# Turning the exponentials of a top-k attention with a transposing DMA in place of TensorE

## The chip, the cores and the metric

The kernel runs on one core of one Trainium2 chip. A core has five engines, each with its own queue of instructions that it works off in order: PE (TensorE, matrix products into PSUM), DVE (VectorE), ACT (ScalarE), POOL (GpSimd) and SP (SyncE, which here only issues transfers). Engines wait for each other through semaphores; sixteen DMA engines move data between the device's memory and the on-chip SBUF. The metric is device time in microseconds (us) of the core, as the median of several runs.

## The reference: what is computed

Two blocks follow each other. The first is attention with 8 batches, 8 heads, 576 rows and a head size of 64, in which each row keeps only its 32 largest scores. The second is a feed-forward block on the 4608 rows of 512 that the first one leaves.

```python
scores = (q @ k.T) / 8                         # per batch and head, 576 x 576
kth    = the 32nd largest score of each row
scores = where(scores >= kth, scores, -1e9)
attn   = exp(scores - max of the row)
attn   = attn / (sum of the row + 1e-9)
x      = attn @ v                              # heads side by side: 4608 x 512
h      = x @ w_in                              # 4608 x 2048
g      = h * sigmoid(1.702 * h)
out    = g @ w_out                             # 4608 x 512
```

All of it is float32.

## The kernel before

The work of the attention is cut into 144 *slots*. A slot is 128 rows of one pair of heads (two tiles of 128 x 576 scores), or, twice per batch, the last 64 rows of two pairs of heads. Each slot goes through these steps: scores on PE; copy to SBUF on ACT; the 32 largest of each row on DVE, in four rounds of eight (8 MAX8 and 6 MATCH_REPLACE8 instructions, 14 in all, over 576 elements each); two small operations for the thresholds on POOL; a Prelu that removes what lies below the threshold, and an Exp that also sums the row, on ACT; the reciprocal on DVE and the division on ACT and POOL; the turning of the 128 x 1152 exponentials on PE, because the product with v needs the keys on the partitions; the product with v on PE. The result, brought from PSUM to SBUF by ACT, is a piece of `xT`. When `xT` has its four pieces (four slots), it goes through the feed-forward block in four groups: `hidden` on PE, `tanh` on ACT, `gate` on POOL, `project` on PE. After the fourth group ACT writes the output tile `ob`, which a DMA stores.

```python
def topk(n):                # returns 14 DVE operations: MAX8 x2, (MATCH_REPLACE8 x2, MAX8 x2) x3
    ...
def bounds(n):              # two small POOL operations: cut, low
    ...
def exponentials(n, between=lambda: None):
    for i in range(2):
        nc.scalar.activation(sc[:, i, :], sc[:, i, :], AF.Prelu, bias=cut[:, i : i + 1], alpha=HUGE)
    between()
    for i in range(2):
        nc.scalar.activation(pr[:, i * S : (i + 1) * S], sc[:, i, :], AF.Exp, bias=low[:, i : i + 1],
                             accum_out=den[:, i : i + 1])

def divide(n):
    nc.vector.tensor_scalar_add(some[:], den[:], 1e-9)
    nc.vector.reciprocal(rden[:], some[:])
    if n < SETTLED:         # SETTLED = 11: the first slots divide while turning
        ...
    else:
        nc.scalar.activation(pr[:, 0:S], pr[:, 0:S], AF.Copy, scale=rden[:, 0:1])
        nc.gpsimd.tensor_scalar(pr[:, S : 2 * S], pr[:, S : 2 * S], rden[:, 1:2], None, op0=ALU.mult)

def turn(n, first, cols, blocks):      # 4 + 4 + 1 blocks per slot
    tp = ps_t.tile([P, 512], F32, name="tp")
    for c in range(blocks):
        nc.tensor.transpose(tp[:, c * P : (c + 1) * P], pr[:, at], ident[:])      # n >= SETTLED
    nc.scalar.copy(out=to, in_=tp[:, 0 : blocks * P])

def hidden():               # PE, 16 products of 128x128 (two passes each): ph <- win, xT
    ...
def tanh(aside):            # ACT: th <- tanh(ph); aside: h <- ph as well, which frees ph
    ...
def gate(aside):            # POOL, two operations (DVE, one, if not aside); takes the newest: gated.pop()
    ...
def project(blocks):        # PE, up to 4 products of 128x512 (two passes each): po += wout, gT
    ...
    if blocks[-1] == G - 1 and g == NG - 1:
        ob = osp.tile([P, C], F32, name="ob")
        nc.scalar.mul(out=ob[:], in_=po[:], mul=0.5 / RAISE**2)
        for on, to in rows:
            nc.sync.dma_start(to, ob[on, :])

# [...]
def two_slots(n):           # from slot 12 on; program order is the order in each engine's queue
    def find(m):
        for i, op in enumerate(topk(m) if live(m) else [lambda: None] * 14):
            op()
            if i == 5 and live(m - 1):
                divide(m - 1)
    def middle(m):
        if len(to_project) > 3:
            project(range(G))
        go = may_project(2 if n < N else 0)
        if go:
            project(range(G - 1))
        turn_main(m)                      # two groups of four blocks
        if go:
            project(range(G - 1, G))
        turn_ends(m)                      # the ninth block

    begin(first)                          # loads
    soften(n - 1)                         # bounds + exponentials
    bring_all()
    tanh(aside)
    find(n)
    gate(aside)
    prepare_some()                        # turns freshly loaded q or k: PE, then ACT
    middle(n - 2)
    hidden()
    begin(second)
    soften(n)
    tanh(aside)
    gate(aside)
    prepare_some()
    middle(n - 1)
    find(n + 1)
    prepare_some()
    for m in (n + 2, n - 2, n - 1, n + 3):
        if m > n: scores(m); copy_scores(m)
        else:     values(m)               # product with v on PE, then ACT brings it to xT
    prepare_some()
    hidden()
```

Buffers that matter: `ph` (the PSUM of `hidden`) has one, the score PSUM holds one slot, the `tp` PSUM (also used by `values` and `prepare`) has two, `pt` (the turned exponentials) two, `sc` (scores in SBUF) three, `pr` two.

Of the kernel before, what the change touches and what calls it, by code (L numbers as in the profile page):

```python
# [11 lines left out]
F32 = mybir.dt.float32  # L12
U32 = mybir.dt.uint32
I32 = mybir.dt.int32
PSUM = bass.MemoryType.PSUM

P = 128
TOPK = 32
# [10 lines left out]
def kernel(  # L29
# [42 lines left out]
    NPIECE = CC * DFF // PIECE + FC  # L72

    FIRST = (TAIL, 0)
    MAIN = (0, FULL + 2 * TAIL)
    SCALE = 1.0 / float(D) ** 0.5


# [11 lines left out]
    loads = pool("loads", 2)  # L90
    vals = pool("vals", 6)
    qkt = pool("qkt", 6)
    scp = pool("scp", 3)
    prp = pool("prp", 2)
    lefts = pool("lefts", 1)
    small = pool("small", 4)
    ptp = pool("ptp", 2)
    dgp = pool("dgp", 1)
    xtp = pool("xtp", 2)
    xtt = pool("xtt", 1)  # L100
    gtp = pool("gtp", 4)
    thp = pool("thp", 2)
    osp = pool("osp", 1)
    ps_s = pool("ps_s", 2, space=PSUM)
    ps_t = pool("ps_t", 2, space=PSUM)
    ps_h = pool("ps_h", 1, space=PSUM)
# [189 lines left out]
    def divide(n):  # L296

        den, pr = st[n]["den"], st[n]["pr"]
        some = small.tile([P, 2], F32, name="some")
        nc.vector.tensor_scalar_add(some[:], den[:], 1e-9)  # L300
        rden = small.tile([P, 2], F32, name="rden")
        nc.vector.reciprocal(rden[:], some[:])
        if n < SETTLED:
            by = st[n]["by"] = dgp.tile([P, 2, P], F32, name="by")
            for i in range(2):
                nc.gpsimd.tensor_scalar(by[:, i, :], ident[:], rden[:, i : i + 1], None, op0=ALU.mult)
        else:
            nc.scalar.activation(pr[:, 0:S], pr[:, 0:S], AF.Copy, scale=rden[:, 0:1])
            nc.gpsimd.tensor_scalar(pr[:, S : 2 * S], pr[:, S : 2 * S], rden[:, 1:2], None, op0=ALU.mult)  # L309

    def turn(n, first, cols, blocks):
        pr = st[n]["pr"]
        if first == 0:
            st[n]["pt"] = ptp.tile([P, 2 * NF + 1, P], F32, name="pt")
        to = st[n]["pt"][:, first : first + blocks, :].rearrange("p c r -> p (c r)")
        tp = ps_t.tile([P, 512], F32, name="tp")
        for c in range(blocks):
            at = slice(cols + c * P, cols + (c + 1) * P)
            if n >= SETTLED:
                nc.tensor.transpose(tp[:, c * P : (c + 1) * P], pr[:, at], ident[:])  # L320
            elif first < 2 * NF:
                nc.tensor.matmul(tp[:, c * P : (c + 1) * P], lhsT=pr[:, at], rhs=st[n]["by"][:, first // NF, :])  # L322
            else:
                for i in range(2):
                    nc.tensor.matmul(
                        tp[i * TAIL : (i + 1) * TAIL, 0:P],
                        lhsT=pr[:, cols + i * TAIL : cols + (i + 1) * TAIL],
                        rhs=st[n]["by"][:, i, :],
                    )
        nc.scalar.copy(out=to, in_=tp[:, 0 : blocks * P])  # L330

    def turn_main(n):
        for i in range(2):
            turn(n, i * NF, MAIN[i], NF)

    def turn_ends(n):

        turn(n, 2 * NF, FULL, 1)

    xts = {}  # L340

    def values(n, put_off=None):

        b, t, hps = slots[n]
        pt = st[n]["pt"]
        outs = []
        for p in range(2 if t == NF else 1):
            cols = slice(p * TAIL, (p + 1) * TAIL) if t == NF else slice(0, P)
            main, tail = vv[b, hps[p]]
            o = ps_t.tile([P, 512], F32, name="o", tag="tp")  # L350
            for c in range(NF + 1):
                for j in range(2):
                    nc.tensor.matmul(  # L353
                        o[j * D : (j + 1) * D, 0 : cols.stop - cols.start],
                        lhsT=main[:, j, c, :] if c < NF else tail[:, j, :],
                        rhs=pt[:, j * NF + c if c < NF else 2 * NF, cols],
                        start=(c == 0),
                        stop=(c == NF),
                    )
            outs.append((o, hps[p]))  # L360
        st[n].clear()

        def bring():
            for o, hp in outs:
                if t < NF:
                    if (b, t) not in xts:
                        xts[b, t] = xtp.tile([P, CC, P], F32, name="xT")
                    nc.scalar.copy(out=xts[b, t][:, hp, :], in_=o[:, 0:P])
                else:
                    if (b // 2, t) not in xts:  # L370
                        xts[b // 2, t] = xtt.tile([P, CC, P], F32, name="xT_t")
                    at = b % 2 * TAIL
                    nc.scalar.copy(out=xts[b // 2, t][:, hp, at : at + TAIL], in_=o[:, 0:TAIL])
            if hps[-1] == NP - 1:
                if t < NF:
                    to = out[b * S : b * S + FULL, :].rearrange("(p t) c -> p t c", t=NF)[:, t, :]
                    ready.append((xts.pop((b, t)), [(slice(0, P), to)]))
                elif b % 2:
                    first = [(b - 1 + i) * S + FULL for i in range(2)]
                    rows = [(slice(i * TAIL, (i + 1) * TAIL), out[x : x + TAIL, :]) for i, x in enumerate(first)]  # L380
                    ready.append((xts.pop((b // 2, t)), rows))

        if put_off is None:
            bring()
        else:
            put_off.append(bring)
# [40 lines left out]
    def gate(aside):  # L427
        if not gated:
            return
        th, h, g, rows = gated.pop()  # L430
        gT = gtp.tile([P, G, P], F32, name="gT")
        if aside:
            nc.gpsimd.tensor_scalar(th[:], th[:], 1.0, None, op0=ALU.add)  # L433
            nc.gpsimd.tensor_tensor(out=gT[:], in0=th[:], in1=h[:], op=ALU.mult)  # L434
        else:
            nc.vector.scalar_tensor_tensor(
                out=gT[:], in0=th[:], scalar=1.0, in1=h[:], op0=ALU.add, op1=ALU.mult
            )
        to_project.append((gT, g, rows))

    def project(blocks):

# [9 lines left out]
                po[:], lhsT=gT[:, i, :], rhs=wout[:, f, :], start=(f == 0), stop=(f == FC - 1)  # L452
            )
        if blocks[-1] == G - 1 and g == NG - 1:
            ob = osp.tile([P, C], F32, name="ob")
            nc.scalar.mul(out=ob[:], in_=po[:], mul=0.5 / RAISE**2)  # L456
            for on, to in rows:
                nc.sync.dma_start(to, ob[on, :])
# [7 lines left out]

    READY = (((-9, -8), (-7, -6), (-4, -3), (-2, -1)), ((-7, -6), (-4, -3), (-3, -2), (-1, -2)))
    FETCH = (((-13, -12), (-11, -10), (-7, -7), (-5, -4)), ((-11, -10), (-9, -8), (-5, -5), (-2, -2)))  # L470
    VALUES = ((-8, -7, 0, 0), (-8, -7, 2, 2))
    by_slot = dict(enumerate([2, 2, 3, 3, 3, 3, 3, 3, 3, 3, 2, 2]))
    for n in by_slot:
        first = sum(map(len, list(by_slot.values())[:n]))
# [179 lines left out]
    def two_slots(n):  # L654
# [11 lines left out]
        def prepare_some():  # L666
            for args in preparing.pop(0):
                prepare(*args)
# [3 lines left out]

        def soften(m):
            if live(m):
                bounds(m)
                exponentials(m)

        def find(m):
            for i, op in enumerate(topk(m) if live(m) else [lambda: None] * 14):
                op()  # L680
                if i == 5 and live(m - 1):
                    divide(m - 1)
                if i > 1 and unfinished:
                    finish_one()

        def middle(m):
            if len(to_project) > 3:
                project(range(G))
            go = may_project(2 if n < N else 0)
            if go:  # L690
                project(range(G - 1))
            if live(m) and "pr" in st[m]:
                turn_main(m)
            if go:
                project(range(G - 1, G))
            if live(m) and "pr" in st[m]:
                turn_ends(m)

        begin(first)
        soften(n - 1)  # L700
        bring_all()
        tanh(aside)
        find(n)
        gate(aside)
        prepare_some()
        middle(n - 2)
        hidden()
        begin(second)
        soften(n)
        tanh(aside)  # L710
        gate(aside)
        prepare_some()
        middle(n - 1)
        find(n + 1)
        prepare_some()
        for m in (n + 2, n - 2, n - 1, n + 3):
            if m > n and live(m):
                scores(m)
                copy_scores(m)
            elif m < n and live(m) and "pt" in st[m]:  # L720
                values(m)
        prepare_some()
        hidden()

    with tc.manual_schedule():
        opening()
        for n in range(SETTLED + 1):
            slot(n)
        for n in range(SETTLED + 1, N + 1, 2):
            two_slots(n)  # L730
        while ready or to_gate or gated or to_project:
            last_slot()
# [30 lines left out]
```

## Time and profile before

The median of three runs is 1610.22 us (1610.13 to 1610.37). The profiled execution spans 1608.6 us at a mean granted TensorE clock of 0.990.

| stretch of the profile | span, us | PE busy | DVE busy | ACT busy | POOL busy |
|---|---|---|---|---|---|
| whole | 1608.6 | 1579.4 | 1471.5 | 1152.5 | 748.0 |
| 400 to 1500 us (steady) | 1100.0 | 1099.5 | 1042.4 | 794.0 | 502.4 |

Busy times overlap, as the engines work beside each other. A matmul is pipelined and its recorded time contains its latency, so a PE that is busy all the time has not necessarily been asked for all it could do; weight loads (PEld) stand for the moment at which PE takes up a matmul. The *releaser* of an idle time is the instruction whose semaphore ended it. Line numbers (L260 and so on) are those of the kernel before.

### The profile page before, as it was taken

The page shows a single profiled execution, that of the slowest core. Times are in us where ns is not written, and L with a number is a line of the kernel's source. Part 1 is how long each engine was busy: PE and PEld are TensorE (multiplying, and loading weights), DVE is VectorE, ACT ScalarE, POOL GpSimd, SP SyncE. Part 2 cuts the span into 40 slices and gives each one's busy share as a digit, 9 for nine tenths or more (in the row PEclk, how much of TensorE's full clock was granted, in tenths as well). Part 3 has the DMA queues.
Part 4 walks back from the last instruction along what each step waited for, and adds up shares of the span by engine and source line. Part 5 has one row for each costly group of instructions (what it writes and reads, how often), then busy time and mean ns, then how long its engine had stood idle before and what let it go on. Part 6 is the DMA issues. An engine that isn't in the chain of part 4 may idle for free.

```text
span 1608.6 us, 32167 instructions
## 1 busy us (share of the span) xinstructions
PE 1579.4 (98%) x12045; PEld 1181.2 (73%) x12045; DVE 1471.5 (91%) x3218; ACT 1152.5 (72%) x2442; POOL 748.0 (46%) x780
## 2 busy tenths in 40 slices
PE   7789999999999999999999999999999999999999
PEld 6666777777777777777777777777777777777776
DVE  7999999999999989999999999999999999999960
ACT  7998777777777777677776777677766777677751
POOL 3887444444444444444344444444444444444430
PEclk7899999999999999999999999999999999999999
DMA  7341111110001001110001000001000100000000
GB/s 238 126 158 50 26 30 30 25 35 3 21 15 45 22 23 30 30 43 17 22 15 45 22 23 29 22 21 34 15 23 15 44 23 23 23 8 8 8 8 14
DMA packets 99100, 56.61 MB, mean 35 GB/s; under 512 B 81536, under 2 KB 90240, under 8 KB 98944
## 3 DMA queue, kind: packets, MB, share of 16 engines
q1 hardware_dynamic: 98512, 54.25, 11.9%
q8 instruction: 95, 1.56, 0.4%
q14 instruction: 61, 0.50, 0.1%
q10 hardware_dynamic: 432, 0.30, 0.1%
HBM read 45.09 MB, written 9.44 MB: 34 GB/s over the span
## 4 chain that ended last, share of the span: by engine, by line
PE 93%; DVE 4%; ACT 3%; POOL 0%; issue 0%; POOLq 0%; ACTq 0%
PE ph L403 32%; PE po L451 31%; PE s_ps L240 10%; PE o L353 10%; PE tp L320 8%; DVE top L260 2%; PE tp L208 2%; DVE left L263 1%; ACT sc L251 1%; PE tp L322 1%; ACT pr L291 0%; PE none L168 0%; ACT raw L152 0%; DVE win L151 0%; ACT pt L330 0%
## 5 line engine op out<-in xcount | busy, mean ns | idle before, releaser
L260 DVE MAX8 top<-left 128x8 f32<-128x576 f32 x864 | 609.4, 747 | 0.0
L451 PE MATMUL po<-wout,gT 128*128 128x512 f32 x1152 | 540.4, 593 | 1.2 <-ACT ob L456 0.7
L403 PEld LDWEIGHTS ph<-xT,win 128*128 128x128 f32 x4096 | 467.7, 192 | 41.2 <-issue 40.5
L403 PE MATMUL ph<-xT,win 128*128 128x128 f32 x4096 | 484.3, 276 | 0.0
L263 DVE MATCH_REPLACE8 left<-top,left 128x576 f32<-128x576 f32 x576 | 423.5, 743 | 0.0
L309 POOL TENSOR_SCALAR pr<-pr,rden 128x576 f32<-128x576 f32 x133 | 230.0, 1729 | 351.4 <-ACT th L420 346.2
L451 PEld LDWEIGHTS po<-wout,gT 128*128 128x128 f32 x1152 | 197.6, 191 | 147.3 <-issue 144.5
L330 ACT COPY pt<-tp 128x512 f32<-128x512 f32 (+1 forms) x432 | 193.1, 481 | 148.6 <-PE tp L320 143.1
L433 POOL TENSOR_SCALAR th<-th 128x512 f32<-128x512 f32 x131 | 196.0, 1496 | 220.8 <-ACT th L420 220.8
L288 ACT ACTIVATE sc<-sc,cut 128x576 f32<-128x576 f32 x288 | 208.1, 773 | 119.5 <-POOL cut L279 119.3
L251 ACT COPY sc<-s_ps 128x576 f32<-128x576 f32 x288 | 169.8, 643 | 70.0 <-PE s_ps L240 69.7
L291 ACT ACTIVATE pr<-sc,low 128x576 f32<-128x576 f32 x288 | 219.1, 764 | 0.0
L320 PEld LDWEIGHTS tp<-ident,pr 128*128 128x128 f32 x1197 | 143.1, 141 | 102.0 <-issue 57.1
L263 DVE MATCH_REPLACE8 left<-top,sc 128x576 f32<-128x576 f32 x288 | 211.6, 742 | 0.0
L260 DVE MAX8 top<-sc 128x8 f32<-128x576 f32 x288 | 202.1, 743 | 2.2 <-ACT sc L251 2.2
L240 PE MATMUL s_ps<-k_t,q_t 64*128 64x288 f32 (+1 forms) x1280 | 183.4, 433 | 0.2 <-ACT k_t L210 0.2
L320 PE MATMUL tp<-ident,pr 128*128 128x128 f32 x1197 | 174.2, 273 | 0.0
L434 POOL TENSOR_TENSOR gT<-th,h 128x512 f32<-128x512 f32 x131 | 167.2, 1276 | 10.9
L353 PE MATMUL o<-pt,v_l 128*64 128x128 f32 (+1 forms) x2560 | 158.3, 267 | 0.7
L353 PEld LDWEIGHTS o<-pt,v_l 128*64 128x64 f32 x2560 | 130.8, 137 | 32.6 <-ACT pt L330 13.5
L240 PEld LDWEIGHTS s_ps<-k_t,q_t 64*128 64x128 f32 (+1 forms) x1280 | 100.0, 179 | 59.4 <-issue 41.5
L279 POOL TENSOR_SCALAR cut<-top 128x2 f32<-128x2 f32 x144 | 39.5, 275 | 219.1 <-DVE top L260 219.1
(66 smaller groups left out, 1166.7 us busy)
## 6 DMA issues: line engine op xcount, KB each, us to landing
q_l<-in_q_dram SPq DMA_DIRECT2D x64, 128.0 KB, 2.9
raw<-in_moe_w_in_dram SPq DMA_DIRECT2D x16, 512.0 KB, 4.7
v_l<-in_v_dram SPq DMA_DIRECT2D x32, 256.0 KB, 3.0
raw<-in_moe_w_out_dram SPq DMA_DIRECT2D x16, 512.0 KB, 3.3
out_dram<-ob SPq DMA_DIRECT2D x32, 256.0 KB, 2.3
k_l<-in_k_dram SPq DMA_DIRECT2D x62, 128.0 KB, 2.9
ends<-in_q_dram SPq DMA_DIRECT2D x32, 32.0 KB, 2.4
v_e<-in_v_dram SPq DMA_DIRECT2D x64, 16.0 KB, 2.5
```

Source lines behind the costliest of these rows:

```text
L240: nc.tensor.matmul(ps[i][rows, c, 0:HALF], lhsT=qT[b, hps[p]][on, cols], rhs=kT[b, hps[p]][on, FIRST[i] + c * HALF : FIRST[i] + (c + 1) * ...
L260: nc.vector.max(top[:, i, 8 * r : 8 * r + 8], (left if r else sc)[:, i, :])
L263: nc.vector.match_replace(left[:, i, :], top[:, i, 8 * r : 8 * r + 8], (left if r else sc)[:, i, :], LOWEST)
L288: nc.scalar.activation(sc[:, i, :], sc[:, i, :], AF.Prelu, bias=cut[:, i : i + 1], alpha=HUGE)
L291: nc.scalar.activation(pr[:, i * S : (i + 1) * S], sc[:, i, :], AF.Exp, bias=low[:, i : i + 1], accum_out=den[:, i : i + 1],)
L309: nc.gpsimd.tensor_scalar(pr[:, S : 2 * S], pr[:, S : 2 * S], rden[:, 1:2], None, op0=ALU.mult)
L320: nc.tensor.transpose(tp[:, c * P : (c + 1) * P], pr[:, at], ident[:])
L330: nc.scalar.copy(out=to, in_=tp[:, 0 : blocks * P])
L353: nc.tensor.matmul(o[j * D : (j + 1) * D, 0 : cols.stop - cols.start], lhsT=main[:, j, c, :] if c < NF else tail[:, j, :], rhs=pt[:, j * N ...
L403: nc.tensor.matmul(ph[:, i, :], lhsT=win[:, c, f * P : (f + 1) * P], rhs=xT[:, c, :], start=(c == 0), stop=(c == CC - 1),)
L433: nc.gpsimd.tensor_scalar(th[:], th[:], 1.0, None, op0=ALU.add)
L451: nc.tensor.matmul(po[:], lhsT=gT[:, i, :], rhs=wout[:, f, :], start=(f == 0), stop=(f == FC - 1))
```

## The change

From slot 11 on PE turns nothing any more. ACT splits each float32 exponential into its two 16-bit halves (the tile of the scores, no longer needed, takes them), a DMA writes the halves to device memory, and a second, transposing DMA, which works on 16-bit elements, reads them back turned: rows alternate between low and high halves, so that the turned pairs stand side by side as float32 again. The purpose is to take the turning off PE and its copies from PSUM off ACT, and to leave the transfers, which are long, two slots of time. Around this the program order of the two-slot loop, the loading times and the buffers were rearranged:

```diff
         else:
-            nc.scalar.activation(pr[:, 0:S], pr[:, 0:S], AF.Copy, scale=rden[:, 0:1])
-            nc.gpsimd.tensor_scalar(pr[:, S : 2 * S], pr[:, S : 2 * S], rden[:, 1:2], None, op0=ALU.mult)
+            for i in range(2):
+                on = slice(i * S, (i + 1) * S)
+                nc.gpsimd.tensor_scalar(pr[:, on], pr[:, on], rden[:, i : i + 1], None, op0=ALU.mult)
 ...
+    def turn_by_dma(n):
+        pr, sc = st[n]["pr"], st[n]["sc"]
+        halves = sc[:].rearrange("p i k -> p (i k)").bitcast(U16).rearrange("p (h k) -> p h k", h=2)
+        nc.scalar.copy(out=halves, in_=pr[:].bitcast(U16).rearrange("p (k h) -> p h k", h=2))
+        rows = apart.tile([P, 2, 2 * S], U16, name="rows")
+        nc.sync.dma_start(rows[:], halves)
+        pt = st[n]["pt"] = ptp.tile([P, 2 * NF + 1, P], F32, name="pt")
+        nc.sync.dma_start_transpose(out=pt[:].bitcast(U16), in_=rows[:].rearrange("q h k -> (q h) k"))
 ...
-        th, h, g, rows = gated.pop()
+        th, h, g, rows = gated.pop(0)
 ...                                        # gate writes into th, no gT; ob shares the buffers of th
         def find(m):
             ...
-                if i == 5 and live(m - 1):
+                if i == 6 and live(m - 1):
                     divide(m - 1)
-        def middle(m): ...
+        def project_one():
+            if may_project(0):
+                project(range(G))
+        def measure(m):
+            if live(m):
+                bounds(m)
+            gate(aside)

         begin(first)
+        project_one()
+        measure(n - 1)
         soften(n - 1)                      # now the exponentials alone
         bring_all()
         tanh(aside)
+        if live(n + 2):
+            scores(n + 2)
+            copy_scores(n + 2)
+        brought = []
+        for m in (n - 4, n - 3):
+            if live(m) and "pt" in st[m]:
+                values(m, brought)
+        if live(n + 3):
+            scores(n + 3)
         find(n)
-        gate(aside)
+        if live(n - 1):
+            turn_by_dma(n - 1)
+        for bring in brought:
+            bring()
+        hidden()
         prepare_some()
-        middle(n - 2)
-        hidden()
+        prepare_some()
         begin(second)
+        project_one()
+        measure(n)
         soften(n)
         tanh(aside)
-        gate(aside)
+        if live(n + 3):
+            copy_scores(n + 3)
         prepare_some()
-        middle(n - 1)
-        find(n + 1)
-        prepare_some()
-        for m in (n + 2, n - 2, n - 1, n + 3): ...
         prepare_some()
         hidden()
+        find(n + 1)
+        if live(n):
+            turn_by_dma(n)
```

`sc` goes from three buffers to four and `th` from two to five; the pools of `gT`, `ob` and the first slots' `by` are given up; `pt` keeps its two buffers, and four tiles of `rows` lie in device memory. READY, FETCH and VALUES, the slots at which q, k and v are loaded and prepared, move by up to three slots, so that nearly all `prepare` calls fall on the two in the middle of a pair of slots. The loop runs two pairs further, to slot 147.

More of the change, by code (lines that the diff above doesn't have):

```diff
@@ L14 @@
 I32 = mybir.dt.int32
+U16 = mybir.dt.uint16
 PSUM = bass.MemoryType.PSUM
+DRAM = bass.MemoryType.DRAM
 P = 128
@@ L74 @@
     FIRST = (TAIL, 0)
-    MAIN = (0, FULL + 2 * TAIL)
+    MAIN = (0, NF + 1)
     SCALE = 1.0 / float(D) ** 0.5
@@ L92 @@
     qkt = pool("qkt", 6)
-    scp = pool("scp", 3)
+    scp = pool("scp", 4)
     prp = pool("prp", 2)
@@ L97 @@
     ptp = pool("ptp", 2)
-    dgp = pool("dgp", 1)
     xtp = pool("xtp", 2)
     xtt = pool("xtt", 1)
-    gtp = pool("gtp", 4)
-    thp = pool("thp", 2)
-    osp = pool("osp", 1)
+    thp = pool("thp", 5)
+    apart = pool("apart", 4, space=DRAM)
     ps_s = pool("ps_s", 2, space=PSUM)
@@ L303, in divide @@
         if n < SETTLED:
-            by = st[n]["by"] = dgp.tile([P, 2, P], F32, name="by")
+            by = st[n]["by"] = xtt.tile([P, 2, P], F32, name="by", tag="xT_t")
             for i in range(2):
@@ L307, in divide, with turn @@
         else:
-            nc.scalar.activation(pr[:, 0:S], pr[:, 0:S], AF.Copy, scale=rden[:, 0:1])
-            nc.gpsimd.tensor_scalar(pr[:, S : 2 * S], pr[:, S : 2 * S], rden[:, 1:2], None, op0=ALU.mult)
-    def turn(n, first, cols, blocks):
+            for i in range(2):
+                on = slice(i * S, (i + 1) * S)
+                nc.gpsimd.tensor_scalar(pr[:, on], pr[:, on], rden[:, i : i + 1], None, op0=ALU.mult)
+    def turn(n, first, blocks):
         pr = st[n]["pr"]
@@ L317, in turn @@
         for c in range(blocks):
[L318 to L322, printed above, removed]
+            at = (first + c) * P
+            if first != NF:
+                by = st[n]["by"][:, first // NF, :]
+                nc.tensor.matmul(tp[:, c * P : (c + 1) * P], lhsT=pr[:, at : at + P], rhs=by)
             else:
@@ L326, in turn @@
                         tp[i * TAIL : (i + 1) * TAIL, 0:P],
-                        lhsT=pr[:, cols + i * TAIL : cols + (i + 1) * TAIL],
+                        lhsT=pr[:, at + i * TAIL : at + (i + 1) * TAIL],
                         rhs=st[n]["by"][:, i, :],
@@ L333, in turn_main @@
         for i in range(2):
-            turn(n, i * NF, MAIN[i], NF)
+            turn(n, MAIN[i], NF)
     def turn_ends(n):
-        turn(n, 2 * NF, FULL, 1)
+        turn(n, NF, 1)
+    def turn_by_dma(n):
[6 more added lines that the diff above has]
+        nc.sync.dma_start_transpose(out=pt[:].bitcast(U16), in_=rows[:].rearrange("q h k -> (q h) k"))
     xts = {}
@@ L355, in values @@
                         lhsT=main[:, j, c, :] if c < NF else tail[:, j, :],
-                        rhs=pt[:, j * NF + c if c < NF else 2 * NF, cols],
+                        rhs=pt[:, MAIN[j] + c if c < NF else NF, cols],
                         start=(c == 0),
@@ L429, in gate @@
             return
-        th, h, g, rows = gated.pop()
-        gT = gtp.tile([P, G, P], F32, name="gT")
+        th, h, g, rows = gated.pop(0)
         if aside:
             nc.gpsimd.tensor_scalar(th[:], th[:], 1.0, None, op0=ALU.add)
-            nc.gpsimd.tensor_tensor(out=gT[:], in0=th[:], in1=h[:], op=ALU.mult)
+            nc.gpsimd.tensor_tensor(out=th[:], in0=th[:], in1=h[:], op=ALU.mult)
         else:
             nc.vector.scalar_tensor_tensor(
-                out=gT[:], in0=th[:], scalar=1.0, in1=h[:], op0=ALU.add, op1=ALU.mult
+                out=th[:], in0=th[:], scalar=1.0, in1=h[:], op0=ALU.add, op1=ALU.mult
             )
-        to_project.append((gT, g, rows))
+        to_project.append((th, g, rows))
     def project(blocks):
@@ L454, in project @@
         if blocks[-1] == G - 1 and g == NG - 1:
-            ob = osp.tile([P, C], F32, name="ob")
+            ob = thp.tile([P, C], F32, name="ob", tag="th")
             nc.scalar.mul(out=ob[:], in_=po[:], mul=0.5 / RAISE**2)
@@ L464, in at @@
         later.setdefault(n, []).append((fn, args))
-    READY = (((-9, -8), (-7, -6), (-4, -3), (-2, -1)), ((-7, -6), (-4, -3), (-3, -2), (-1, -2)))
-    FETCH = (((-13, -12), (-11, -10), (-7, -7), (-5, -4)), ((-11, -10), (-9, -8), (-5, -5), (-2, -2)))
-    VALUES = ((-8, -7, 0, 0), (-8, -7, 2, 2))
+    READY = (((-9, -8), (-7, -6), (-4, -3), (-2, -1)), ((-8, -7), (-6, -5), (-4, -3), (-4, -3)))
+    FETCH = (((-13, -12), (-11, -10), (-7, -7), (-5, -4)), ((-12, -11), (-10, -9), (-6, -6), (-5, -5)))
+    VALUES = ((-8, -7, 2, 2), (-8, -7, 3, 3))
     by_slot = dict(enumerate([2, 2, 3, 3, 3, 3, 3, 3, 3, 3, 2, 2]))
@@ L674, in soften @@
             if live(m):
-                bounds(m)
                 exponentials(m)
@@ L684, in find @@
                     finish_one()
-        def middle(m):
-            if len(to_project) > 3:
+        def project_one():
+            if may_project(0):
                 project(range(G))
[L689 to L697, printed above, removed]
+        def measure(m):
+            if live(m):
+                bounds(m)
+            gate(aside)
         begin(first)
+        project_one()
+        measure(n - 1)
         soften(n - 1)
@@ L702, in two_slots @@
         tanh(aside)
-        find(n)
-        gate(aside)
+        if live(n + 2):
[7 more added lines that the diff above has]
+            scores(n + 3)
+        find(n)
+        if live(n - 1):
[3 more added lines that the diff above has]
+        hidden()
         prepare_some()
-        middle(n - 2)
-        hidden()
+        prepare_some()
         begin(second)
+        project_one()
+        measure(n)
         soften(n)
         tanh(aside)
-        gate(aside)
+        if live(n + 3):
+            copy_scores(n + 3)
         prepare_some()
-        middle(n - 1)
-        find(n + 1)
-        prepare_some()
[L716 to L721, printed above, removed]
         prepare_some()
         hidden()
+        find(n + 1)
+        if live(n):
+            turn_by_dma(n)
     with tc.manual_schedule():
@@ L728 @@
             slot(n)
-        for n in range(SETTLED + 1, N + 1, 2):
+        for n in range(SETTLED + 1, N + 4, 2):
             two_slots(n)
```

## The prediction, made before the changed kernel ran

> **What bounds the kernel now.** I read first the busy times, the clock and the chain of waits, then DVE's own waits, then the timeline of one pair of slots.
>
> ```profile
> span 1608.6 us, 32167 instructions
> PE 1579.4 (98%) x12045; PEld 1181.2 (73%) x12045; DVE 1471.5 (91%) x3218; ACT 1152.5 (72%) x2442; POOL 748.0 (46%) x780
> ...
> PEclk7899999999999999999999999999999999999999
> ...
> PE 93%; DVE 4%; ACT 3%; POOL 0%; issue 0%; POOLq 0%; ACTq 0%
> ...
> L320 PE MATMUL tp<-ident,pr 128*128 128x128 f32 x1197 | 174.2, 273 | 0.0
> ```
> ```profile
> DVE some L300 <- ACT pr L291: 75.0, 68, 3.3
> ```
>
> PE carries 93% of the chain and is never without work from 120 us on. DVE is close behind: its only steady wait is at the reciprocal (L300), for ACT's sum of the row, 75.0 us in all. The table of stages counts 131 slots between 160 and 1550 us, 10.61 us per slot. One slot of DVE alone, read off the timeline from the first MAX8 at 799.39 to that of the next slot at 809.64, is 10.25 us, with L300 lengthened by 0.33 to 0.50 while it waits; the next slot takes 10.61 with a wait of 0.60. That leaves 9.92 and 10.01: **9.95 us** is DVE's floor. So freeing PE can bring at most 10.61 - 9.95 = 0.66 us per slot, over the 132 slots from slot 12 on 87 us.
>
> The rows of the timeline that give the pitches (start, duration, engine):
>
> ```profile
> 806.70 0.85 PEld L353 LDWEIGHTS o<-pt,v_l 128*64 128x64 f32 x16 [0.39 <-ACT pr L308]
> ...
> 809.03 0.79 PEld L240 LDWEIGHTS s_ps<-k_t,q_t 64*128 64x128 f32 x8 [0.17 <-issue]
> ...
> 810.20 3.65 PEld L403 LDWEIGHTS ph<-xT,win 128*128 128x128 f32 x32 [0.39 <-issue]
> ...
> 811.43 1.45 ACT L288 ACTIVATE sc<-sc,cut 128x576 f32<-128x576 f32 x2
> ...
> 813.77 0.30 PEld L451 LDWEIGHTS po<-wout,gT 128*128 128x128 f32 x2
> ...
> 814.42 0.17 DVE L300 TENSOR_SCALAR some<-den 128x2 f32<-128x2 f32 x1 [0.60 <-ACT pr L291]
> 814.62 0.17 DVE L302 RECIPROCAL rden<-some 128x2 f32<-128x2 f32 x1
> ...
> 814.99 1.73 POOL L309 TENSOR_SCALAR pr<-pr,rden 128x576 f32<-128x576 f32 x1 [4.80 <-ACT th L420]
> ```
> ```profile
> 1548.01 1.02 PE L451 MATMUL po<-wout,gT 128*128 128x512 f32 x2
> ...
> 1549.07 0.60 ACT L456 ACTIVATE ob<-po 128x512 f32<-128x512 f32 x1 [0.22 <-PE po L451]
> 1549.57 0.26 ACT L330 COPY pt<-tp 128x128 f32<-128x128 f32 x1
> ```
>
> From start to start on PE: two `values` 2.33 (806.70 to 809.03), `scores` 1.17, `hidden` 3.57; eight passes of `project` 3.44 (the chain's row "3.44 PE po L451 x8"). On ACT: Prelu to the end of the reciprocal 811.43 to 814.79, 3.36 us; POOL starts 0.2 later; ACT takes up `ob` 0.04 after the last product's end and is free 0.5 later.
>
> **What the skill says.** "DMA: Bandwidth & Descriptors" (section "DMA Transpose (X-bar)") admits only 2-byte elements, hence the halves; its section "Latency and other measured facts" gives 261 GB/s for a transposing DMA. A slot is 128 x 1152 x 4 bytes, 590 KB: an estimate of 2.3 us. No trace here shows such a transfer yet. "ScalarE: Activation LUTs" ("What ACT_TABLE_LOAD costs") gives one element per cycle, 0.833 ns, plus about 0.19 us fixed, and an overlap of 0.09 between neighbours; the trace agrees on the overlap (an Exp of 0.77 us lets the next start 0.67 later) and has a little more fixed (512 elements from SBUF at L152 take 0.685, so 0.25). "TensorE: Matmul & The Clock Gate" (table of specifications) says that ScalarE, VectorE and GpSimd are strict FIFOs: one waiting instruction holds all behind it. The trace agrees: DVE stands still at L300 although the next MATCH_REPLACE8 needs nothing from it. Its part 1 says that an idle window of 3.4 us halves PE's clock; before, the stage from 20 to 30 us, with PE busy 4.44 of 10, was granted 0.50.
>
> **The change part by part, per slot from 11 on.** PE loses 9 transposes: in the pair above about 2.2 us per pair, 1.1 per slot. ACT loses three copies of `pt` (0.54 + 0.54 + 0.2) and one division (0.69), together 2.0, and gains a split of 2304 elements: 2304 x 0.833 + 0.25 = 2.17, estimated, a pitch of 2.07. POOL gains a second division, 1.73. DVE is unchanged. By busy time alone this would be the 87 us. But the order in the queues changes too, and there I choose to follow the chain.
>
> ACT's queue around the middle of a pair is now: split of n-1, two brings of `values`, the copies of `prepare`, then `ob` if the second `project` closes an output tile, and only then Prelu and Exp of slot n, for whose sum DVE waits. PE's queue is: project, scores, two values, scores, hidden, prepare, project, hidden. A tile takes four slots, so pairs alternate: an *opening* pair, whose first `hidden` needs the two pieces just brought, and a *closing* pair, whose second `project` ends in `ob`.
>
> Count from the end of the reciprocal in the first half of an opening pair. POOL divides twice: 0.2 + 1.73 + 0.08 + 1.73 = 3.74. Split, to 5.86. Brings at a pitch of 0.17, the last ending at 6.3. Prelu to reciprocal 3.36: 9.57, under DVE's 9.95, so DVE leads here. PE: the first `hidden` has its last pieces at 6.4 and frees PE at 9.5; project 12.95; hidden 16.5; in the closing pair project 19.95, scores 21.1, values 23.45, scores 24.6, hidden 28.2; the last product ends 3.7 later, 31.9; `ob` 0.5; then 3.36 more: **35.8**. DVE had its three slots done at 29.9. With 9.95 to the next opening pair the cycle of four slots is 45.75, or **11.44 per slot**, though PE has work for only 37.4 of it (4 x 3.57 + 4 x 3.44 + 4 x 1.17 + 2 x 2.33): it stands idle about 3 us before the opening `hidden` and 4.7 before the closing pair's last `hidden`, whose PSUM the `tanh` behind the Exp frees.
>
> Even with PE far ahead the closing pair can't do it in 9.95: after the reciprocal tanh, h and two score copies take 1.7, then scores 1.17, hidden 3.6, project 3.7, ob 0.5, 3.36: 14.1.
>
> `prepare` adds: in opening pairs its transposes stand behind `hidden`, so ACT waits until 10.3 and copies 0.5 (q) to 1.3 (q and k); the reciprocal comes at 14.2 to 15.0, `tanh` and the next `hidden` follow it, and the cycle grows by 2.3 to 3.2. Per 36 slots (two batches, nine cycles) five opening pairs have one, 15.9 us; three closing pairs 1.5 each, 4.5; the double `values` and `scores` of the short slots 3.5. So 9 x 45.75 + 23.9 = 435.7 us per 36 slots, **12.1 per slot**, against 10.61: +1.49 x 132 = +197 us.
>
> End: before, 51.6 us pass from the last reciprocal (1557.0) to 1608.6. Now the last values come two slots later; PE still has, after them, 4 hidden and 7 project (38.4 us), then `ob` and a store, about 62: +10. Slots 0 to 10 stay: 0. Sum: 1610 + 197 + 10 = **1817**; I say 1820.
>
> **The rivals.**
> *PE is freed and DVE becomes the bound*: 1610 - 87 + 10 = about 1535, 4 to 5% faster. For it speaks that PE holds 93% of the chain and that 75 us of DVE's waits are for ACT. Against it: ACT's FIFO puts a wait for PE ahead of DVE's sum every second pair, which before stood elsewhere (ACT waited only 22.1 us for all 36 `ob`).
> *The transposing DMA is the bound*: SP's queue is in order, `pt` has two buffers, and a slot's transfer waits for the values of two slots before. A write (about 3 us, as stores of 256 KB land in 2.3) and a transfer per slot must fit into half the 23 us between the values of two pairs. At 2.3 us they do; at 10 us just; at 15 the pair would take over 30 us and the kernel 2300 or more. Nothing in the trace before measures it; DMA engines were only 11.9% busy, so bandwidth is there.
> *PE goes cold*: idle stretches of 3 to 5 us in each cycle may halve the clock for some us; 1 us per cycle would be +33, 3 us +100, up to 1920.
>
> **Range and chances.** The floor of the chain (9.95 x 3 + 14.1 = 43.95 per four slots, plus preparation 2.65) gives 11.65 per slot, 1610 + 137 + 10 = 1757; with cooler hops or a cold PE 1900. I take 1745 to 1900. Faster needs the queue order to be read wrongly by me: 0.05. Within 2%: 0.03. Slower: 0.92.
>
> **What would show it.** Right: DVE's waits at the reciprocal grow from 75 to about 250 us, in steps of 4 to 6 at every second pair; ACT waits for PE before `ob` for well over 100 us in all; PE falls to near 85% busy in the steady part, waiting for ACT; the stretch between two closing pairs is 45 to 49 us; the split takes 2.1 to 2.2; transfers land within 10 us and PE hardly waits for DMA at `values`. Wrong: DVE without waits (order misread), PE idle for DMA before `values` (transfer is the bound), a clock well under 0.95 in the steady part (cold PE), or a split of 3 us or more.

## The result, and the profile after

| | us, median | ratio to before, 95% interval |
|---|---|---|
| before | 1610.18 (1608.6 to 1610.37) | |
| after | 1820.83 (1820.16 to 1822.16) | 1.131 [1.1295, 1.1327] |

The kernel is 13% slower. The page of after: span, busy time, share and number of instructions of each engine; the granted clock in 40 slices; the chain that ended last; then groups (busy time and mean ns of one | idle time before them and its releaser), and two rows of DMA issues (KB each, us to landing).

```profile
span 1820.4 us, 29720 instructions
...
PE 1563.9 (86%) x10848; PEld 1140.0 (63%) x10848; DVE 1449.2 (80%) x3220; ACT 1151.6 (63%) x2042; POOL 969.0 (53%) x909
...
PEclk8898899999999998999999998899999999899999
...
PE 53%; DVE 24%; ACT 15%; POOL 6%; issue 2%; POOLq 0%; DVEq 0%; ACTq 0%
...
L344 ACT COPY sc<-pr 128x2304 uint16<-128x2304 uint16 x133 | 281.1, 2114 | 220.3 <-POOL pr L310 220.2
...
rows<-sc SPq DMA_DIRECT2D x133, 576.0 KB, 2.8
...
pt<-rows SPq DMA_TRANSPOSE x133, 4.6
```

No engine is full any more: PE fell from 98% to 86%, DVE from 91% to 80%, and the chain, which was 93% PE, now passes from engine to engine. Such a page suggests that a round trip sets the time. Which one, the list of waits tells (us in total, times, the longest):

```profile
DVE some L300 <- ACT pr L291: 294.1, 56, 12.1
...
ACT ob L465 <- PE po L460: 198.9, 36, 13.2
PEld ph L413 <- ACT h L433: 192.1, 44, 5.3
```

DVE waits 294.1 us at the reciprocal where it had waited 75.0. ACT waits for PE ahead of each of the 36 output tiles, 5.5 us in the mean. PE waits for ACT to free `ph`. No wait of PE's `values` for a transfer stands in the list. The timeline of one closing pair (start, duration, idle before and its releaser) shows how the three hang together:

```profile
939.53 3.65 PEld L413 LDWEIGHTS ph<-xT,win 128*128 128x128 f32 x32 [0.38 <-issue]
...
943.21 3.60 PE L460 MATMUL po<-wout,th 128*128 128x512 f32 x8
...
946.84 0.60 ACT L465 ACTIVATE ob<-po 128x512 f32<-128x512 f32 x1 [5.82 <-PE po L460]
947.34 1.43 ACT L288 ACTIVATE sc<-sc,cut 128x576 f32<-128x576 f32 x2
...
950.31 0.17 DVE L300 TENSOR_SCALAR some<-den 128x2 f32<-128x2 f32 x1 [5.76 <-ACT pr L291]
...
951.28 5.14 PEld L413 LDWEIGHTS ph<-xT,win 128*128 128x128 f32 x32 [5.31 <-ACT h L433]
```

`ob` waits for the last product; Prelu (L288), whose threshold POOL had ready at 940.2, stands behind it in ACT's queue; DVE waits 5.76 us for the sum; `tanh` and the copy of `h` come behind the Exp, so PE in turn has been idle 5.31 us when `ph` comes free. The loop closes in the next opening pair: the pieces of `xT` that PE's first `hidden` needs stand behind the split in ACT's queue, and the split waits for POOL's division and so for DVE's reciprocal. PE waits 1.39 us for them (the line at 966.56 under run 7).

Each slot has one row of L300, and a table of stages counts 33 of them in each of 400 to 800, 800 to 1200 and 1200 to 1600 us: **12.12 us per slot** against 10.61 before. From the start of one reciprocal to the next it is 9.90 in three of four slots and 15.2 to 15.8 in the slot with the output tile, unless a preparation or a short slot is near.

### The profile page after: what moved, and what is told of

It reads as the page before. It is cut to its first block, busy times and chain, and to the rows that moved or that the text cites. A ratio compares the mean times of both kernels' runs of the same rounds, so it can differ in the third digit from the quotient of the medians.

```text
span 1820.4 us, 29720 instructions
## 1 busy us (share of the span) xinstructions
PE 1563.9 (86%) x10848; PEld 1140.0 (63%) x10848; DVE 1449.2 (80%) x3220; ACT 1151.6 (63%) x2042; POOL 969.0 (53%) x909
## 3 DMA queue, kind: packets, MB, share of 16 engines
q1 hardware_dynamic: 428352, 211.17, 42.5%
q8 instruction: 85, 1.39, 0.3%
## 4 chain that ended last, share of the span: by engine, by line
PE 53%; DVE 24%; ACT 15%; POOL 6%; issue 2%; POOLq 0%; DVEq 0%; ACTq 0%
PE ph L413 22%; PE po L460 18%; DVE top L260 12%; DVE left L263 10%; PE o L363 6%; POOL pr L310 5%; PE s_ps L240 5%; ACT pr L291 5%; ACT sc L344 3%; ACT sc L288 2%; ACT ob L465 1%; ACT q_t L210 1%; PE tp L208 1%; PE tp L322 1%; ACT th L430 1%
## 5 line engine op out<-in xcount | busy, mean ns | idle before, releaser
L310 POOL TENSOR_SCALAR pr<-pr,rden 128x576 f32<-128x576 f32 x266 | 457.1, 1728 | 563.1 <-ACT th L430 408.8
L413 PE MATMUL ph<-xT,win 128*128 128x128 f32 x4096 | 565.5, 302 | 162.7 <-ACT h L433 137.8
L413 PEld LDWEIGHTS ph<-xT,win 128*128 128x128 f32 x4096 | 540.0, 215 | 236.2 <-ACT h L433 170.9
L460 PE MATMUL po<-wout,th 128*128 128x512 f32 x1152 | 519.7, 594 | 0.7 <-ACT ob L465 0.7
L344 ACT COPY sc<-pr 128x2304 uint16<-128x2304 uint16 x133 | 281.1, 2114 | 220.3 <-POOL pr L310 220.2
L460 PEld LDWEIGHTS po<-wout,th 128*128 128x128 f32 x1152 | 209.6, 192 | 211.0 <-issue 209.2
L300 DVE TENSOR_SCALAR some<-den 128x2 f32<-128x2 f32 x144 | 23.4, 163 | 294.3 <-ACT pr L291 294.1
L288 ACT ACTIVATE sc<-sc,cut 128x576 f32<-128x576 f32 x288 | 207.4, 771 | 2.0 <-POOL cut L279 1.9
L240 PE MATMUL s_ps<-k_t,q_t 64*128 64x288 f32 (+1 forms) x1280 | 193.4, 451 | 7.1 <-ACT sc L251 6.9
L443 POOL TENSOR_TENSOR th<-th,h 128x512 f32<-128x512 f32 x129 | 164.9, 1278 | 10.7
L465 ACT ACTIVATE ob<-po 128x512 f32<-128x512 f32 x36 | 21.5, 597 | 198.9 <-PE po L460 198.9
```

The costliest lines, as they stand in the source:

```text
L240: nc.tensor.matmul(ps[i][rows, c, 0:HALF], lhsT=qT[b, hps[p]][on, cols], rhs=kT[b, hps[p]][on, FIRST[i] + c * HALF : FIRST[i] + (c + 1) * ...
L310: nc.gpsimd.tensor_scalar(pr[:, on], pr[:, on], rden[:, i : i + 1], None, op0=ALU.mult)
L344: nc.scalar.copy(out=halves, in_=pr[:].bitcast(U16).rearrange("p (k h) -> p h k", h=2))
L413: nc.tensor.matmul(ph[:, i, :], lhsT=win[:, c, f * P : (f + 1) * P], rhs=xT[:, c, :], start=(c == 0), stop=(c == CC - 1),)
L460: nc.tensor.matmul(po[:], lhsT=gT[:, i, :], rhs=wout[:, f, :], start=(f == 0), stop=(f == FC - 1))
```

## The experiments

All times are medians, with the kernel before measured on the same chip (1610.07 for the first four runs, 1610.3 for the last three). The ratios are to before.

### 1. The output tile behind the softmax

The theory: 9.95 us is DVE's floor, and what lies above it is `ob` standing ahead of Prelu (mainly), and the preparation's copies standing ahead of it too. This run moves the write of `ob` in ACT's queue behind the Exp, `tanh` and the copies of scores.

```diff
     def project(blocks, wait=False):
         # [...]
-            ob = thp.tile([P, C], F32, name="ob", tag="th")
-            nc.scalar.mul(out=ob[:], in_=po[:], mul=0.5 / RAISE**2)
-            # [stores]
+            obs.append(write)          # the same three lines, in a function
+            if not wait:
+                write_out()
     # two_slots: project_one() passes wait=True, and
     copy_scores(n + 2)                 # and likewise after copy_scores(n + 3)
+    write_out()
```

> The changed kernel, but the output tile ob is written by ScalarE after the Exp, tanh and score copies of its half of the pair, not ahead of the Prelu. Theory (ScalarE's queue: a wait for PE stands ahead of the sums that VectorE needs): the closing pairs lose their step at the reciprocal; per 36 slots 9 x 39.6 plus 22 for preparation in opening pairs, 10.5 in closing ones and 7 for the short slots is 396 us, 11.0 per slot, so about 1673 us (1640 to 1700). Rival, the transposing transfer bounds the kernel: the order of ob changes nothing, 1815 to 1825. Rival, the longer division on GpSimd and the split bound the loop of exponentials: the stall moves to the next reciprocal, gain under 30 us. Rival, the cold PE: PE's idle stretch before the last hidden of a closing pair goes with the wait, so a gain of at most 33 cycles x 1.7 = 56 us.

Measured: **1648.36** (1646.92 to 1652.05), ratio 1.0247 [1.0231, 1.0262]. Moving one instruction of 0.6 us takes off 172 us. Waits of this kernel:

```profile
DVE some L300 <- ACT pr L291: 124.3, 49, 7.4
...
ACT ob L473 <- PE po L466: 34.2, 20, 13.2
```

DVE's wait falls from 294.1 to 124.3 us, by 170, which is the whole gain. So the place of `ob` was the larger part of the loss. The three rivals fall with this: a bound by the transfers or by the exponentials would have left 1790 us or more, a cold PE at least 1765.

### 2. The preparation behind the softmax

The transposes and copies that prepare fresh q and k go from the first half of a pair, where they stand ahead of Prelu, to the second half; `ob` stays where the change put it.

```diff
         hidden()
-        prepare_some()
-        prepare_some()
         begin(second)
         # [...]
             copy_scores(n + 3)
-        prepare_some()
-        prepare_some()
+        for _ in range(4):
+            prepare_some()
         hidden()
```

> The changed kernel, but all calls of prepare stand after the score copies of the second half, so that ScalarE's copies of prepare come after the Exp of the slot; ob stays where it is. Theory: the steps of 4.1 to 4.6 us in opening pairs go, the closing ones stay; PE still carries the cycle, so only about 1 us per slot-pair with preparation is won: 426.7 us per 36 slots, 11.85 per slot, about 1785 us (1765 to 1805). Transfer-bound or loop-bound: no change.

Measured: **1789.36** (1788.72 to 1791.1), ratio 1.1121 [1.1105, 1.1138]: 31 us less than after. Its waits:

```profile
DVE some L300 <- ACT pr L291: 260.0, 52, 12.4
ACT ob L465 <- PE po L460: 243.4, 36, 13.2
```

The reciprocal's wait falls by 34, but the wait ahead of `ob` grows from 198.9 to 243.4: what one cause leaves, the other takes up in part. That is why removing one alone understates it.

### 3. Both

> Both moves together. Theory: VectorE is the bound but for the short slots and small delays of the split, 366.9 us per 36 slots, 10.2 per slot, about 1566 us (1545 to 1600): faster than the kernel before, and more than the two gains added (148 + 36), because each alone leaves the other wait in the same cycle. Waits at the reciprocal fall from 294 us to under 60. Transfer-bound: 1800 or more. Loop-bound (division twice on GpSimd, split): about 1750.

Measured: **1573.4** (1571.59 to 1577.25), ratio 0.978 [0.9761, 0.9799]. It takes off 247 us, where the two alone add up to 172 + 31 = 204, and it is 2.2% faster than the kernel before. Waits of this kernel:

```profile
ACT sc L251 <- DMA rows<-sc: 54.0, 34, 3.7
...
DVE some L300 <- ACT pr L291: 48.8, 36, 3.8
ACT ob L473 <- PE po L466: 38.1, 23, 13.2
```

From 400 to 800 us it has 39 rows of L300 and from 800 to 1200 us 40, 10.1 us per slot, and most steps are DVE's 9.90. The transfers are those of after, yet now 54 us of waits for the store of the rows show up: with less slack elsewhere a transfer begins to be seen.

### 4. The transposing transfer twice

The rival: the transfers set the pace. Each slot's transposing DMA is issued twice, with the same source and destination.

```diff
-        nc.sync.dma_start_transpose(out=pt[:].bitcast(U16), in_=rows[:].rearrange("q h k -> (q h) k"))
+        for _ in range(2):
+            nc.sync.dma_start_transpose(out=pt[:].bitcast(U16), in_=rows[:].rearrange("q h k -> (q h) k"))
```

> The changed kernel with every transposing transfer issued twice, into the same tile, one after the other: nothing else changes. Theory: the transfers lie beside other work and PE doesn't wait for them, so 1821 to 1840 us. Transfer-bound: 4.6 us more per slot, 133 slots, about 2430 us.

Measured: **1939.12** (1932.58 to 1943.53), ratio 1.2047 [1.2013, 1.208]. Neither expectation holds: 118 us more than after, 0.89 us per slot. SP's queue shows what a second transfer takes of it; first a line of after, then one of this kernel:

```profile
937.38 2.65 SPq L348 DMA_TRANSPOSE pt<-rows  x1
```
```profile
940.54 7.16 SPq L349 DMA_TRANSPOSE pt<-rows  x2
```

And the waits of this kernel, SP's own and then those of the engines:

```profile
SPq L349 <- DMA pt<-rows: 289.2, 133, 3.6
```
```profile
DVE some L300 <- ACT pr L291: 413.0, 65, 14.1
...
ACT sc L251 <- DMA rows<-sc: 203.2, 55, 8.4
```

One issue holds SP for about 2.5 us. The second has to wait for the first to land, so the pair holds it for 7, or 4.5 us more per slot. If SP's queue set the pace, 4.5 x 133 = some 600 us would have been added; it was a fifth of that. So the transfer of after isn't the bound, but I was wrong that it has room to spare. What gives way first, by the trace, is ACT (PE's `values` wait for `pt` as well, but 31.0 us in all): the store of the rows stands behind the transfers in SP's queue (it is issued 3.8 us after the split in the mean, where in after it was 0.34), and the copy of fresh scores has to wait for that store, which reads the `sc` buffer that the copy fills. With it waits all that stands behind it on ACT. Whether another queue or a fifth `sc` buffer alone would take these 118 us away wasn't tried.

### 5. One PSUM tile for the short slots' values

The kernel of run 3, in whose timeline steps above 9.90 stand at the short slots (up to 12.5 us) and at the preparations. The two products of a short slot's `values` now share one PSUM tile.

```diff
-            o = ps_t.tile([P, 512], F32, name="o", tag="tp")
+            if p == 0:
+                both = ps_t.tile([P, 512], F32, name="o", tag="tp")
+            o = both[:, p * P : (p + 1) * P]
```

> This is the kernel with both reorderings (1573.4 us), with one thing more: the two products of the short slot share one PSUM tile instead of taking two. Theory: in that kernel the steps between reciprocals are 9.90 us nearly everywhere, and the rest sits at the short slots (steps of 11.83 to 12.17 us), where TensorE waits for a PSUM tile, and at the preparations. Without the second tile I expect some 5 us less per 36 slots, over about four rounds of 36 slots about 19 us: about 1555 us, range 1545 to 1565, and the reciprocals' wait below 40 us from 48.8. Rival: the short slots' stalls come from the copies of the transposed input that the values need, whichever tile they use; then the time stays at 1568 to 1578.

Measured: **1553.64** (1550.01 to 1555.11), ratio 0.9651 [0.9635, 0.9667], the fastest kernel of this study, 20 us under run 3. Its reciprocal's wait:

```profile
DVE some L300 <- ACT pr L291: 26.4, 18, 3.2
```

18 waits in the place of 36, and the steps at the short slots are 9.91 now; those that are left above 10.5 (10.8 to 12.9) stand where q and k are prepared. So the tile, and not the copies of the piece of `xT`, was what the short slots waited for.

### 6. The order of run 3 with the turning on PE

Does the gain come from the DMA, or from the order, which the kernel before might have had as well? Here TensorE turns again; scores, projection, output tile and preparation stand as in run 3, POOL still does both divisions (in the kernel before ACT did one), and `pt` has a third buffer in place of a fourth `sc`.

```diff
-        nc.scalar.copy(out=halves, in_=pr[:].bitcast(U16).rearrange("p (k h) -> p h k", h=2))
-        # [rows, the store and the transposing DMA]
+        for first, blocks in ((0, NF), (NF, NF), (2 * NF, 1)):
+            tp = ps_t.tile([P, 512], F32, name="tp")
+            for c in range(blocks):
+                at = (first + c) * P
+                nc.tensor.transpose(tp[:, c * P : (c + 1) * P], pr[:, at : at + P], ident[:])
+            to = pt[:, first : first + blocks, :].rearrange("p c r -> p (c r)")
+            nc.scalar.copy(out=to, in_=tp[:, 0 : blocks * P])
     # two_slots: the brings of the values stand ahead of the turning, not behind it
```

> The order is that of the kernel with both reorderings (1573.4 us: scores, projection and output writes placed the same), but TensorE turns the exponentials again, with nine transposes and three ScalarE copies a slot, in place of the split, the store of rows and the transposing DMA. Theory: the gain is the DMA's, and the new order only lets it show. TensorE then has some 1.1 us a slot more, 41.8 us of work in four slots where VectorE has 39.6, and it waits for GpSimd's division besides: at least 10.45 us a slot, 1620 to 1680 us in all. Rival: the order alone is the gain, and the kernel before would have had it as well: 1573 us or less.

Measured: **1688.51** (1688.12 to 1688.71), ratio 1.0485 [1.047, 1.0501]. The rival (this order alone) falls: with PE turning, it is 115 us slower than with the DMA, and slower than the old one. But it is also above what I expected, and one stretch of its timeline says why:

```profile
905.87 1.27 ACT L350 COPY pt<-tp 128x512 f32<-128x512 f32 x3 [5.28 <-PE tp L348]
907.04 1.44 ACT L288 ACTIVATE sc<-sc,cut 128x576 f32<-128x576 f32 x2
...
910.03 0.17 DVE L300 TENSOR_SCALAR some<-den 128x2 f32<-128x2 f32 x1 [1.82 <-ACT pr L291]
```

Prelu stands behind another copy that waits for PE. The reciprocals come alternately 9.91 and 11.82 us apart in the undisturbed pairs, 10.87 in the mean, where PE's work alone would have asked for 10.45. So the run isn't the best that PE could do; the kernel before is better ordered for it. How much another order could give it wasn't tried. By the prediction's own figures it would be little: 10.61 us per slot stand against the 10.45 of PE's work, 0.16 us, or an estimated 21 us over 132 slots.

### 7. Keeping PE warm

In after the `hidden` behind the 5.31 us of idle takes 5.14 us, not 3.65. Is this on the path? 20 products, which nothing reads, fill the gap in each closing pair.

```diff
         project_one()
+        if live(n) and n % 4 == 0:
+            none = ps_t.tile([P, 512], F32, name="tp")
+            for i in range(20):
+                nc.tensor.matmul(none[:, 0:P], lhsT=ident[:], rhs=ident[:], start=True, stop=True)
         measure(n)
```

> The changed kernel (1820.8 us) with 20 products of 128 by 128 more, which nothing reads, on TensorE between the second projection and the measure of each closing pair, to fill the 4.5 to 5.3 us for which TensorE is idle there, so that the hidden products behind run at the higher clock. Theory: the hidden products behind the idle stretch take about 3.65 us in place of 5.1 to 5.3, but the 1.6 us were absorbed by a later wait of TensorE, so the time stays within 0.5 per cent: 1812 to 1830 us. Rival: the cold TensorE lies on the path; then about 33 times 1.7 us come off, to about 1765 us.

Measured: **1842.95** (1842.58 to 1847.43), ratio 1.1451 [1.1434, 1.1468]: 22 us *more* than after, which neither expected. The opening `hidden` of after, and then three rows of this kernel:

```profile
966.56 3.20 PEld L413 LDWEIGHTS ph<-xT,win 128*128 128x128 f32 x28 [1.39 <-ACT xT L378]
```
```profile
929.68 3.20 PEld L414 LDWEIGHTS ph<-xT,win 128*128 128x128 f32 x28 [2.88 <-ACT xT L379]
...
959.88 3.65 PEld L414 LDWEIGHTS ph<-xT,win 128*128 128x128 f32 x32 [0.21 <-ACT h L434]
...
975.16 4.83 PEld L414 LDWEIGHTS ph<-xT,win 128*128 128x128 f32 x28 [2.87 <-ACT xT L379]
```

The products do what they are for: the closing `hidden` at 959.88 takes 3.65. And what this wins is indeed absorbed: the wait of the opening `hidden` for the pieces of `xT` grows from 1.39 to 2.87 us, by 1.48, and in the cycle ahead of it four reciprocals take 45.47 us with the products and without. So the rival falls. But the idle time, moved there, makes PE cold there: from 400 to 1600 us 14 opening `hidden` take 4.73 to 4.83 us in place of 3.20, and most of these *are* on the path, for the slot's `tanh` and what follows wait for them. Reciprocal by reciprocal, this kernel falls behind after in 13 steps of 1.5 to 1.6 us, each in the pair of a cold opening `hidden` or in the closing pair behind it; after the last of the 144 slots it is 20.2 us behind.

## Why the prediction was right

The mechanism was right, and so was the time (1820 predicted, 1820.83 measured). That the two agree to within 1 us is luck, as three of the terms below were off by 2.4 to 6.4 us in 36 slots and nearly cancel. By the prediction's own steps:

- **PE and ACT are freed, DVE's floor is 9.95.** Right: 9.90 is the step between most reciprocals of after. (PE was not quite without a pause from 120 us on: between 140 and 160 us it was busy for 18.5 of 20.) What the change was meant for is there, and pays only in runs 3 and 5.
- **ACT's queue holds Prelu behind `ob`; DVE waits there.** Right, and shown by run 1: 172 of the 211 us go with the place of that one instruction. The page "TensorE: Matmul & The Clock Gate" (table of specifications) says that ScalarE's queue is a strict FIFO; Prelu at 947.34, right behind an `ob` that had waited 5.82, agrees.
- **The cycle of four slots, 45.75.** 45.47 and 45.48 in the two cycles without preparation (reciprocals at 905.04, 950.51 and 995.99). The closing step of it is 15.8, where 15.9 was predicted (35.8 less two slots of 9.95).
- **Preparation and short slots, 20.4 and 3.5 per 36 slots.** Both mis-sized, and with the shorter cycle (2.5 us less in nine) they nearly cancel. The two cycles with short slots, 1095.19 to 1146.04 to 1195.98, have no preparation and take 50.85 and 49.94 us: that is 9.9 per 36 slots for the short slots, and what is left for the preparation is 18. Of the short slots I had counted PE's work only, not the wait for a PSUM tile, which run 5 shows in the order of run 3. Together the 36 slots from 658.17 to 1095.19 take 437.0 us against 435.7.
- **The last reciprocal, +197.** It starts at 1752.87 in place of 1556.87: +196.0.
- **The tail, +10.** 67.3 us in place of 51.6 (from the reciprocal's end): +15.8. (The loop runs one pair of slots further, to slot 147, and not two.) Here 62 was predicted; the 3 us that I rounded up covered half of the rest.
- **The split, 2.17 us.** 2.11.
- **The rival "DVE becomes the bound" (1535).** It fell for this order, but its logic is what run 5 comes near to (1553.64), once `ob` and the preparation stand behind the softmax.
- **The rival "the transfer is the bound".** It fell: run 4 added a fifth of what a bound would have. The estimate of 2.3 us from "DMA: Bandwidth & Descriptors" ("Latency and other measured facts", 261 GB/s) was too low, though: 4.6 us to landing, 590 KB in 4.6 us or 128 GB/s with all fixed time in it. The measurement decides.
- **The rival "PE goes cold" (+33 to +100).** It happens in the closing pairs (5.1 to 6.5 us where 3.65 is the warm time; the clock is 0.93 in the whole), but costs nothing there, as run 7 shows. I had put 3 us of idle ahead of the opening `hidden`; 1.25 to 1.39 are left of it, and the cold clock took the rest.

## What to carry to other kernels

When work is taken off the fullest engine, read each queue in its new order and ask of every instruction that waits for another engine what stands behind it: one evacuation of 0.6 us, put ahead of a softmax that everything waits for, cost 172 us here, of the 211 that the changed kernel had lost. Remove suspected waits together as well as alone, since each hides part of the other (172 and 31 alone, 247 together). An engine's idle time that is absorbed isn't slack for the taking: fill it, and it may reappear where it counts.

## What the runs showed of the hardware

- A transposing DMA of 590 KB landed in 4.6 us, and its issue alone held SP's queue for 2.5 us in the median (2.25 at least); the plain store of the same bytes held it for 0.34 and landed in 2.8. With each transposing DMA issued twice (run 4), the store behind them was issued late, while a transposing DMA still landed in 4.6 us and the DMA queue rose from 42.5% to 59.1% of the 16 engines. By these figures what ran short first was the issuing queue and the order in it, not the bytes.
- PE's clock fell after idle stretches shorter than I had reckoned with. In run 7 PE was without a product for 2.69 us ahead of the opening `hidden` at 929.69, which stayed at full clock, and for 2.68 ahead of that at 975.16, which was granted 0.50 from 976.05 us on. The clock record of the trace tells what decides. All 50 changes of the granted clock between 200 and 1700 us lie on one grid of 3.413 us. Of the intervals of this grid that ran at full clock, the 25 in which PE was without a product for 2.03 us or more in sum were followed by the lower clock, and none of the 387 with 1.84 us or less. The first stretch lies across the end of an interval, so that 1.26 and 1.43 us of it fall into two; of the second, 2.52 us fall into one (interval, its length, PE busy, granted clock, DMA share and GB/s):

```profile
924.85:928.26 3.41, 2.15 (x20) 1.00 0.87 174
928.26:931.68 3.42, 1.99 (x17) 1.00 0.66 190
972.64:976.05 3.41, 0.89 (x8) 1.00 0.80 193
976.05:979.46 3.41, 3.41 (x19) 0.50 0.38 149
```

  In after the border lies between 1.92 us (344 intervals below) and 2.03 us (39 above); in run 4 it is less sharp, with both outcomes between 1.51 and 1.98 us. "TensorE: Matmul & The Clock Gate" (part 1) has a free-running window of about 3.4 us, with which the grid agrees. It lets the clock fall after an idle window; here some 2 us without a product within one were enough.
